# Banded attention with a mixture of experts: pair outputs scaled in place in PSUM, two small steps given to ScalarE, operand turns placed behind later filler pieces

## The chip, the cores and the metric

The kernel runs on one core of a Trainium2 chip. The metric is the time of one execution in microseconds on the device. The runs of the kernel before gave 2286.73 us (median of 3; 2285.66 to 2288.38).

The engines are named as the profile names them: PE is TensorE (PEld its weight loads), DVE is VectorE, ACT is ScalarE, POOL is GpSimd, SP is SyncE. A matrix product leaves its result in PSUM; SBUF is the other on-chip memory.

## The reference, cut to what matters

```python
def _attn_ref(q, k, v, n_global, n_local):        # q, k, v: 4 x 8 x 768 x 64; n_global 8, n_local 96
    scores = q @ k^T / sqrt(D) + bias(head, distance)      # masked to a band of 96 keys and 8 global keys
    scores = scores - max(scores, axis=-1)
    a = exp(scores)
    a = a / (sum(a, axis=-1) + 1e-09)
    return a @ v

def _moe_ref(x, w_gate, w1, w2):                  # x: 3072 x 512; 8 experts, 512 x 1024 x 512 each
    logits = x @ w_gate
    P = exp(logits - logits.max())
    for _ in range(8):                            # Sinkhorn: rows, then columns, are brought to one sum
        P /= P.sum(1) + 1e-09; P /= P.sum(0) + 1e-09; P *= N / E
    return sum(P[:, e:e+1] * (relu(x @ w1[e]) @ w2[e]) for e in range(8))
```

## The kernel before, in words

The first 380 us or so are the attention stage, in eight units of 384 query rows. A unit holds four pairs of heads, a pair three tasks (one block of 128 query rows for both heads), and the code goes through the tasks two at a time, as a chunk. In a chunk (`Banded.unit`, L352 on) PE gets, in an order that is fixed by hand: the scores of the two tasks that lie four and five ahead (`ahead`, `scores`), the value products of the two tasks of the chunk before (`flush`), the transposes of two softmax blocks (`turn`, tiles `t_ps`), and then pieces of other work. `between(n)` puts in pieces of the dense first expert for the unit before (`filler`, three matmuls each into `h_ps` or `y_ps`, and the gate into `g_ps`); unit 0 has none. Between the pieces stand two calls of `prepare` (the operand turns: tiles `tp`, transposes of raw queries and keys, split by L239 on ACT into a high part `qh`/`kh` and by L240 on DVE into a low part `ql`/`kl`) and, in two chunks of three, `invert` (tile `r_ps`, transposes of the pair's inverse sums, read back by L393 on DVE). All of `tp`, `t_ps` and `r_ps` take turns in two PSUM buffers.

Outside PE the order is set by the scheduler of the framework; each engine runs its list strictly in order.

After the third task of a pair, `softmax` makes the inverse sums: add epsilon to six sums per partition (L294, DVE), reciprocal (L295, DVE), spread them to 128x384 (L297, DVE). When a pair's value products are done, `flush` scales them (L382, DVE, out of PSUM into the SBUF tile `inv`), takes the high part (L384, ACT, from SBUF) and the low part (L385, DVE, both inputs in SBUF). There are 32 pairs, so each of these lines runs 32 times.

The gate's logits leave PSUM by L719 and L720 (DVE), once for each of the units 0 to 6 in this stage; the matmul piece behind them waits for the buffer.

On POOL, `sums_of` and `differences` combine the finished units of a pair of units: 25 instructions of 128x768 in a row, three times (once for units 0 and 1, once for 2 and 3, once for 4 and 5). After the attention stage follows the mixture of experts, on PE nearly without a gap, to the end.

The change touches `softmax`, `unit` and `flush`. The functions with their line numbers:

Of the kernel before, what the change touches and what calls it, by code (L numbers as in the profile page):

```python
# [12 lines left out]
ALU = mybir.AluOpType  # L13
# [4 lines left out]
P = 128  # L18
# [4 lines left out]
EPS = 1e-9  # L23
UT = 3
# [4 lines left out]
AHEAD = 4  # L29
CHUNK = 2  # L30
# [58 lines left out]
class Banded:  # L89
# [178 lines left out]
    def softmax(self, t, s_list):  # L268


        nc, D = self.nc, self.D
        n, group = divmod(t, len(GROUPS))
        _, half, g = self.work[n]
        blocks = self.key_blocks(half)[1]
        p_sb = self.wrk.tile([P, 2, 2, P], F32, name="p_sb")
        mx = self.wrk.tile([P, 2], F32, name="mx", bufs=4)
        if group == 0:
            self.sums[n] = self.wrk.tile([P, UT, 2], F32, name="sm", bufs=4)
        sm = self.sums[n]
        views = []  # L280
        for u, (j, i) in enumerate(GROUPS[group]):
            h = 2 * g + j
            nb = len(blocks[i])
            bias = self.bias0[:, h] if nb == 1 else self.bias1[:, h]
            pv = p_sb[:, u, 0:nb].rearrange("p a c -> p (a c)")
            views.append(pv)
            nc.vector.tensor_tensor_reduce(out=pv, in0=s_list[u], in1=bias, scale=-(D ** -0.5), scalar=3.0e38,
                                           op0=ALU.add, op1=ALU.min, accum_out=mx[:, u:u + 1])
        for u, pv in enumerate(views):
            j, i = GROUPS[group][u]  # L290
            nc.scalar.activation(out=pv, in_=pv, func=AF.Exp, bias=mx[:, u:u + 1], scale=-1.0,
                                 accum_out=sm[:, i, j:j + 1])
        if group == len(GROUPS) - 1:
            nc.vector.tensor_scalar(out=sm, in0=sm, scalar1=EPS, scalar2=None, op0=ALU.add)  # L294
            nc.vector.reciprocal(out=sm, in_=sm)  # L295
            self.inv[n] = self.wrk.tile([P, UT, P], F32, name="inv", bufs=3)
            nc.vector.tensor_copy(self.inv[n].rearrange("p t (j d) -> p (t j) d", j=2),  # L297
                                  sm.rearrange("p t j -> p (t j)").unsqueeze(2).broadcast_to([P, 2 * UT, D]))
        return p_sb

    def blocks(self, n, group):
# [28 lines left out]
    def unit(self, u, xh, xl, between):  # L330

        NG, per = len(GROUPS), len(GROUPS) * (self.H // 2)
        if u == 0:
            self.load_qk(1)
            self.load_v(1)
            for t in range(NG):
                self.prepare(t)
            self.scale_bias(0)  # L340
            self.keep_warm(self.ps, "o", WARM0)
            self.ahead(range(0, CHUNK))
            for t in range(NG, 2 * NG):
                self.prepare(t)
            for g in range(1, self.H // 2):
                self.scale_bias(g)
            for t in range(CHUNK, AHEAD, CHUNK):
                self.ahead(range(t, t + CHUNK))
            for t in range(2 * NG, AHEAD + NG + 1):
                self.prepare(t)  # L350
        for t in range(u * per, (u + 1) * per, CHUNK):
            self.ahead(range(t + AHEAD, t + AHEAD + CHUNK))  # L352
            self.flush()
            turned = [(t + c, self.turn(t + c)) for c in range(CHUNK)]
            between(CHUNK)
            for c in range(CHUNK):
                self.prepare(t + AHEAD + NG + 1 + c)
                between(1)
            for t1, pT in turned:
                n, group = divmod(t1, NG)  # L360
                if group == NG - 1:
                    self.invert(n)
                if group == 0:
                    self.outs[n] = self.ps.tile([P, UT, P], F32, name="o_ps", tag="o", bufs=2)
                g = n % (self.H // 2)
                self.pending.append((n, group, pT, self.outs[n], xh[:, g], xl[:, g]))

    def flush(self):


        ended = None
        for n, group, pT, o_ps, xh, xl in self.pending:
            self.values(n, group, pT, o_ps)
            if group == len(GROUPS) - 1:
                ended = n, o_ps, xh, xl
        self.pending = []
        if ended is None:
            return
        n, o_ps, xh, xl = ended
        self.load_v(n + 2)  # L380
        xf = self.inv.pop(n)
        self.nc.vector.tensor_tensor(out=xf, in0=o_ps, in1=xf, op=ALU.mult)  # L382
        xf = xf.rearrange("p t c -> p (t c)")
        self.nc.scalar.copy(out=xh, in_=xf)  # L384
        self.nc.vector.tensor_tensor(out=xl, in0=xf, in1=xh, op=ALU.subtract)  # L385

    def invert(self, n):

# [645 lines left out]
```

## Time and profile before

| | |
|---|---|
| runs of the kernel | 2286.73 us median of 3 (2285.66 to 2288.38) |
| the profiled execution | 2288.16 us |
| its span, first to last instruction | 2286.3 us |
| PE busy | 2236.0 us (98%) |
| DVE busy | 1560.3 us (68%) |
| ACT busy | 696.2 us (30%) |
| POOL busy | 823.5 us (36%) |
| mean granted TensorE clock | 0.989 |

The busy shares are means over two stages that differ. The page's picture of 40 slices shows it: ACT is busy 4 to 6 tenths in the first seven slices and 2 in the others, and the clock is below 9 tenths only in the first slice. In the rows below, a number in brackets behind an instruction is the idle time of its engine just before it and what ended that. A clock of 1.00 is 2.4 GHz, of 0.50 is 1.2 GHz.

### The profile page before, as it was taken

The numbers are of one execution on the slowest core, as the hardware profiler recorded it, in microseconds if no ns is written. First come the engines' busy times: TensorE is split into PE (matmuls) and PEld (weight loads), VectorE is DVE, ScalarE is ACT, GpSimd is POOL, SyncE is SP. The second block draws the span as 40 slices with busy tenths as digits, with TensorE's granted clock in tenths as the row PEclk, the third lists the DMA queues.
The fourth block names the chain that finished last, engine by engine and source line by source line (L and its number), as shares of the span: only waits on it lengthen the run. The fifth ranks groups of instructions, "written<-read, shape, count | busy, mean of one in ns | idle before, by whom it ended". The sixth has DMA issues, their size and how long they took to land.

```text
span 2286.3 us, 31486 instructions
## 1 busy us (share of the span) xinstructions
PE 2236.0 (98%) x12147; PEld 1991.2 (87%) x12147; DVE 1560.3 (68%) x2746; ACT 696.2 (30%) x1528; POOL 823.5 (36%) x655
## 2 busy tenths in 40 slices
PE   7989989999999999999999999999999999999998
PEld 5777878898998998998998998998998999989987
DVE  6566666886766666766666667666766666666665
ACT  5655654332222222222222224222222222222221
POOL 4165283432333333333333234333333233333320
PEclk8999999999999999999999999999999999999999
DMA  6455433110111011111001361101110101110101
GB/s 163 116 163 145 125 85 95 32 43 28 37 38 38 28 30 36 38 37 37 28 29 38 129 239 39 36 28 38 37 38 28 37 28 38 37 37 28 35 22 57
DMA packets 177615, 133.75 MB, mean 59 GB/s; under 512 B 117040, under 2 KB 148784, under 8 KB 177456
## 3 DMA queue, kind: packets, MB, share of 16 engines
q1 hardware_dynamic: 177456, 131.65, 19.3%
q8 instruction: 97, 1.59, 0.3%
q14 instruction: 62, 0.51, 0.1%
HBM read 108.81 MB, written 22.81 MB: 58 GB/s over the span
## 4 chain that ended last, share of the span: by engine, by line
PE 90%; DVE 3%; issue 3%; POOL 2%; ACT 1%; DMA 0%; SPq 0%; DVEq 0%; POOLq 0%; ACTq 0%
PE y_ps L686 15%; PE y_ps L687 15%; PE y_ps L685 14%; PE bank_d L618 4%; PE bank_d L617 4%; PE bank_c L617 4%; PE bank_c L619 4%; PE bank_a L618 4%; PE bank_c L618 4%; PE bank_a L617 4%; PE bank_d L619 4%; PE bank_a L619 4%; PE bank_b L617 2%; PE bank_b L619 2%; PE bank_b L618 2%
## 5 line engine op out<-in xcount | busy, mean ns | idle before, releaser
L937 DVE SCALAR_TENSOR_TENSOR acc<-y_ps,pm,acc 128x512 f32<-128x512 f32 x672 | 500.2, 748 | 327.0 <-PE y_ps L687 324.5
L687 PE MATMUL y_ps<-w2h,hh 128*128 128x512 f32 x1440 | 567.5, 394 | 0.0
L686 PE MATMUL y_ps<-w2h,hl 128*128 128x512 f32 x1440 | 566.9, 394 | 0.0
L685 PE MATMUL y_ps<-w2l,hh 128*128 128x512 f32 x1440 | 561.9, 390 | 0.0
L538 POOL TENSOR_TENSOR w2l<-w2f,w2h 128x1024 fp32r<-128x1024 f32 x60 | 144.5, 2408 | 702.0 <-ACT w2h L537 702.0
L687 PEld LDWEIGHTS y_ps<-w2h,hh 128*128 128x128 f32 x1440 | 270.1, 188 | 53.7
L685 PEld LDWEIGHTS y_ps<-w2l,hh 128*128 128x128 f32 x1440 | 270.4, 188 | 43.5 <-DVE acc L937 0.2
L686 PEld LDWEIGHTS y_ps<-w2h,hl 128*128 128x128 f32 x1440 | 270.0, 188 | 43.4
L560 POOL TENSOR_TENSOR wsum<-w1f 128x256 f32<-128x256 f32 x300 | 225.5, 786 | 216.5 <-DMA w1f<-in_moe_w_dram 216.5
L538 POOL TENSOR_TENSOR wl<-wsum,wh 128x1280 fp32r<-128x1280 f32 x60 | 177.4, 2957 | 279.4 <-ACT wh L537 279.4
L625 ACT ACTIVATE hh<-h 128x384 fp32r<-128x384 f32 x120 | 63.1, 526 | 502.5 <-DVE h L665 501.1
L626 DVE SCALAR_TENSOR_TENSOR hl<-t,hh 128x384 fp32r<-128x384 f32 x120 | 165.1, 1376 | 10.2 <-ACT hh L625 10.1
L617 PE MATMUL bank_d<-xl,wh 128*128 128x384 f32 x480 | 160.9, 335 | 1.5 <-DVE t L671 1.5
L617 PE MATMUL bank_c<-xl,wh 128*128 128x384 f32 x480 | 161.9, 337 | 0.0
L619 PE MATMUL bank_c<-xh,wh 128*128 128x384 f32 x480 | 161.9, 337 | 0.0
L618 PE MATMUL bank_c<-xh,wl 128*128 128x384 f32 x480 | 161.2, 336 | 0.0
L618 PE MATMUL bank_d<-xh,wl 128*128 128x384 f32 x480 | 161.2, 336 | 0.0
L618 PE MATMUL bank_a<-sh,wl 128*128 128x384 f32 x480 | 161.1, 336 | 0.0
L617 PE MATMUL bank_a<-sl,wh 128*128 128x384 f32 x480 | 161.0, 335 | 0.0
L619 PE MATMUL bank_a<-sh,wh 128*128 128x384 f32 x480 | 160.8, 335 | 0.0
L619 PE MATMUL bank_d<-xh,wh 128*128 128x384 f32 x480 | 160.3, 334 | 0.0
L626 DVE SCALAR_TENSOR_TENSOR hl<-h,hh 128x384 fp32r<-128x384 f32 x120 | 110.1, 918 | 68.7 <-ACT hh L625 68.7
(195 smaller groups left out, 3960.1 us busy)
## 6 DMA issues: line engine op xcount, KB each, us to landing
w1f<-in_moe_w_dram SPq DMA_DIRECT2D x62, 512.0 KB, 3.4
w2f<-in_moe_w_dram SPq DMA_DIRECT2D x62, 512.0 KB, 3.7
out_dram<-acc SPq DMA_DIRECT2D x24, 256.0 KB, 2.2
ys<-y_sb SPq DMA_DIRECT2D x21, 256.0 KB, 2.1
acc<-ys SPq DMA_DIRECT2D x7, 768.0 KB, 4.3
acc<-in_q_dram SPq DMA_DIRECT2D x32, 96.0 KB, 2.5
acc<-in_k_dram SPq DMA_DIRECT2D x32, 96.0 KB, 2.7
acc<-in_v_dram SPq DMA_DIRECT2D x32, 96.0 KB, 2.2
```

The costliest lines, as they stand in the source:

```text
L538: self.nc.gpsimd.tensor_tensor(out=lo, in0=full, in1=hi, op=ALU.subtract)
L560: nc.gpsimd.tensor_tensor(out=s[:, n], in0=x, in1=y, op=op)
L617: self.pe.matmul(out, lhsT=hi(c), rhs=xlo(c), start=(first and c == 0), stop=False, skip_group_check=True)
L618: self.pe.matmul(out, lhsT=lo(c), rhs=xhi(c), start=False, stop=False, skip_group_check=True)
L619: self.pe.matmul(out, lhsT=hi(c), rhs=xhi(c), start=False, stop=(last and c == n - 1), skip_group_check=True)
L625: nc.scalar.activation(out=hh, in_=src, func=AF.Relu)
L626: self.latest = nc.vector.scalar_tensor_tensor(out=hl, in0=src, scalar=0.0, in1=hh, op0=ALU.max, op1=ALU.subtract)
L685: self.pe.matmul(y_ps, lhsT=hh[:, cols], rhs=lf, start=(f == 0), stop=False)
L686: self.pe.matmul(y_ps, lhsT=hl[:, cols], rhs=wf, start=False, stop=False)
L687: self.pe.matmul(y_ps, lhsT=hh[:, cols], rhs=wf, start=False, stop=(f == n - 1))
L937: nc.vector.scalar_tensor_tensor(out=a, in0=y_ps, scalar=moe.pm[:, tt, e:e + 1], in1=a, op0=ALU.mult, op1=ALU.add)
```

## The change

Three edits. In `softmax` the addition of epsilon and the spreading of the inverse sums go from DVE to ACT; the reciprocal stays on DVE. In `flush` the product with the inverse sums is written back into the PSUM tile `o_ps`, and both halves of the split read it from there. In `unit` the two calls of `prepare` stand behind `invert` and behind one more piece each.

```diff
@@ softmax
-            nc.vector.tensor_scalar(out=sm, in0=sm, scalar1=EPS, scalar2=None, op0=ALU.add)
+            nc.scalar.add(sm, sm, EPS)
             nc.vector.reciprocal(out=sm, in_=sm)
             self.inv[n] = self.wrk.tile([P, UT, P], F32, name="inv", bufs=3)
-            nc.vector.tensor_copy(self.inv[n].rearrange("p t (j d) -> p (t j) d", j=2),
-                                  sm.rearrange("p t j -> p (t j)").unsqueeze(2).broadcast_to([P, 2 * UT, D]))
+            nc.scalar.copy(out=self.inv[n].rearrange("p t (j d) -> p (t j) d", j=2),
+                           in_=sm.rearrange("p t j -> p (t j)").unsqueeze(2).broadcast_to([P, 2 * UT, D]))
@@ unit
             turned = [(t + c, self.turn(t + c)) for c in range(CHUNK)]
             between(CHUNK)
-            for c in range(CHUNK):
-                self.prepare(t + AHEAD + NG + 1 + c)
-                between(1)
             for t1, pT in turned:
...
                 self.pending.append((n, group, pT, self.outs[n], xh[:, g], xl[:, g]))
+            for c in range(CHUNK):
+                between(1)
+                self.prepare(t + AHEAD + NG + 1 + c)
@@ flush
-        xf = self.inv.pop(n)
-        self.nc.vector.tensor_tensor(out=xf, in0=o_ps, in1=xf, op=ALU.mult)
-        xf = xf.rearrange("p t c -> p (t c)")
-        self.nc.scalar.copy(out=xh, in_=xf)
-        self.nc.vector.tensor_tensor(out=xl, in0=xf, in1=xh, op=ALU.subtract)
+        self.nc.vector.tensor_tensor(out=o_ps, in0=o_ps, in1=self.inv.pop(n), op=ALU.mult)
+        of = o_ps.rearrange("p t c -> p (t c)")
+        self.nc.scalar.copy(out=xh, in_=of)
+        self.nc.vector.tensor_tensor(out=xl, in0=of, in1=xh, op=ALU.subtract)
```

From L385 on, the line numbers of the kernel after are smaller by one (L240 and L295 keep theirs; the scaling is L381, the high part L383, the low part L384, the read-back of the inverse sums L392, the logits L718 and L719, the low part of an expert's hidden values L625).

What this makes of the engines' lists is shown at three places. The first is DVE in the chunk of unit 1 in which the gate's logits leave PSUM, from the end of one pair on (the same seven times in the stage). Before:

```order
L382 TENSOR_TENSOR inv<-o_ps,inv 128x384
L294 TENSOR_SCALAR sm<-sm 128x6
L295 RECIPROCAL sm<-sm 128x6
L297 COPY inv<-sm 128x384
L385 TENSOR_TENSOR xl<-inv,xh 128x384
L719 COPY lg<-gt_ps 128x24
L720 TENSOR_TENSOR lg<-gt_ps,lg 128x24
L626 SCALAR_TENSOR_TENSOR hl<-h_ps,hh 128x384
L240 TENSOR_TENSOR ql<-tp,qh 128x384
L240 TENSOR_TENSOR kl<-tp,kh 128x512
L393 COPY inv<-r_ps 128x384
```

And with the change:

```order
L381 TENSOR_TENSOR o_ps<-o_ps,inv 128x384
L384 TENSOR_TENSOR xl<-o_ps,xh 128x384
L295 RECIPROCAL sm<-sm 128x6
L392 COPY inv<-r_ps 128x384
L718 COPY lg<-gt_ps 128x24
L625 SCALAR_TENSOR_TENSOR hl<-h_ps,hh 128x384
L719 TENSOR_TENSOR lg<-gt_ps,lg 128x24
L240 TENSOR_TENSOR ql<-tp,qh 128x384
L240 TENSOR_TENSOR kl<-tp,kh 128x512
```

Two instructions are gone, the read-back of the inverse sums stands ahead of the logits, and `hl` between their two halves (in the built program the next piece on PE waits for this `hl`, where it waited for the second half).

The second place is PE in the same chunk, from the last matmul of a piece to the next scores. Before:

```order
L83 MATMUL h_ps<-xh,w1h 128x384
L86 MATMUL tp<-ident,acc 128x128 x3
L86 MATMUL gt_ps<-ident,g_sb 128x16 x3
L83 MATMUL h_ps<-xl,w1h 128x384
L83 MATMUL h_ps<-xh,w1l 128x384
L83 MATMUL h_ps<-xh,w1h 128x384
L86 MATMUL tp<-ident,acc 128x128 x4
L83 MATMUL h_ps<-xl,w1h 128x384
L83 MATMUL h_ps<-xh,w1l 128x384
L83 MATMUL h_ps<-xh,w1h 128x384
L86 MATMUL r_ps<-ident,inv 128x128 x3
```

And with the change:

```order
L83 MATMUL h_ps<-xh,w1h 128x384
L86 MATMUL r_ps<-ident,inv 128x128 x3
L86 MATMUL gt_ps<-ident,g_sb 128x16 x3
L83 MATMUL h_ps<-xl,w1h 128x384
L83 MATMUL h_ps<-xh,w1l 128x384
L83 MATMUL h_ps<-xh,w1h 128x384
L86 MATMUL tp<-ident,acc 128x128 x3
L83 MATMUL h_ps<-xl,w1h 128x384
L83 MATMUL h_ps<-xh,w1l 128x384
L83 MATMUL h_ps<-xh,w1h 128x384
L86 MATMUL tp<-ident,acc 128x128 x4
```

The transposes of the inverse sums have changed places with the operand turns, and the last turn stands right ahead of the scores.

The third place is PE one chunk earlier, in front of scores of which the second task reads keys that were turned in this chunk (16 chunks of 48 are of this kind). Before:

```order
L86 MATMUL t_ps<-ident,p_sb 128x128 x8
L86 MATMUL tp<-ident,raw_745 128x128 x4
L83 MATMUL g_ps<-xl,ghl 128x384
...
L83 MATMUL g_ps<-xh,ghl 128x384
L86 MATMUL tp<-ident,raw_745 128x128 x2
L83 MATMUL h_ps<-xl,w1h 128x384
L83 MATMUL h_ps<-xh,w1l 128x384
L83 MATMUL h_ps<-xh,w1h 128x384
L86 MATMUL r_ps<-ident,inv 128x128 x3
L83 MATMUL s_ps_1042<-kl,qh 128x256
```

And with the change:

```order
L86 MATMUL t_ps<-ident,p_sb 128x128 x8
L86 MATMUL r_ps<-ident,inv 128x128 x3
L83 MATMUL g_ps<-xl,ghl 128x384
...
L83 MATMUL g_ps<-xh,ghl 128x384
L86 MATMUL tp<-ident,raw_751 128x128 x4
L83 MATMUL h_ps<-xl,w1h 128x384
L83 MATMUL h_ps<-xh,w1l 128x384
L83 MATMUL h_ps<-xh,w1h 128x384
L86 MATMUL tp<-ident,raw_751 128x128 x2
L83 MATMUL s_ps_1042<-kl,qh 128x256
```

The turn of four key blocks has moved behind the gate's piece; one piece and a turn of two blocks are left between it and the scores. In the built program the seventh score matmul waits for the `kl` of the four-block turn, not for that of the two-block one.

From the end of the attention stage on, the lists of all engines are the same but for a few neighbours in the first tens of microseconds.

## Rows read from the trace of the kernel before

**Rows 1.** Busy time by stage (PE, PEld, DVE, ACT, POOL; clock, DMA).

```profile
20.00:80.00 60.00, 47.06 (x380) 37.35 (x379) 38.86 (x125) 36.37 (x114) 17.83 (x15) 0.85 0.62 154
80.00:380.00 300.00, 276.18 (x2230) 237.21 (x2229) 191.84 (x552) 174.03 (x517) 141.95 (x77) 0.95 0.46 124
380.00:2286.00 1906.00, 1898.33 (x9473) 1709.07 (x9471) 1317.15 (x2015) 477.95 (x876) 653.16 (x539) 1.00 0.14 45
```

**Rows 2.** The same view, stretches of the attention stage with and without POOL.

```profile
105.00:153.00 48.00, 40.52 (x315) 34.43 (x315) 34.00 (x84) 24.46 (x75) 46.40 (x25) 0.90 0.58 171
153.00:198.00 45.00, 44.42 (x377) 38.47 (x374) 26.60 (x96) 30.02 (x92) 0.03 (x1) 0.99 0.48 127
...
290.00:338.00 48.00, 40.45 (x315) 34.57 (x315) 33.96 (x83) 24.27 (x74) 46.35 (x25) 0.90 0.31 75
```

**Rows 3.** Who PE waited for, 80 to 380 us (us in total, times, longest).

```profile
PE h_ps L83 <- DVE lg L720: 12.2, 6, 3.5
PE r_ps L86 <- DVE ql L240: 5.6, 3, 2.0
PE t_ps L86 <- DVE kl L240: 4.3, 3, 2.0
```

**Rows 4.** DVE in order of time, 300.5 to 307 us, POOL busy (start, us).

```profile
300.56 1.01 DVE L294 TENSOR_SCALAR sm<-sm 128x6 f32<-128x6 f32 x1 [0.31 <-ACT p_sb L291]
...
301.82 1.70 DVE L297 COPY inv<-sm 128x384 f32<-128x384 f32 x1
303.44 2.15 DVE L385 TENSOR_TENSOR xl<-inv,xh 128x384 fp32r<-128x384 f32 x1
...
305.82 0.55 DVE L626 SCALAR_TENSOR_TENSOR hl<-h_ps,hh 128x384 fp32r<-128x384 f32 x1
```

**Rows 5.** DVE in order of time, 168.6 to 170.6 us, POOL idle.

```profile
168.63 0.17 DVE L294 TENSOR_SCALAR sm<-sm 128x6 f32<-128x6 f32 x1
...
169.06 0.36 DVE L297 COPY inv<-sm 128x384 f32<-128x384 f32 x1
170.00 0.56 DVE L385 TENSOR_TENSOR xl<-inv,xh 128x384 fp32r<-128x384 f32 x1 [0.58 <-ACT xh L384]
```

**Rows 6.** PE in order of time: two of the gaps under POOL.

```profile
243.01 0.55 PE L86 MATMUL r_ps<-ident,inv 128*128 128x128 f32 x3 [1.54 <-DVE ql L240]
...
306.05 0.66 PE L83 MATMUL h_ps<-xl,w1h 128*128 128x384 f32 x1 [3.48 <-DVE lg L720]
```

**Rows 7.** Busy time and clock (the last but two numbers: clock) around and behind them.

```profile
240.00:250.00 10.00, 8.46 (x67) 6.51 (x67) 8.05 (x20) 6.06 (x18) 5.83 (x4) 1.00 0.81 217
...
306.05:312.00 5.95, 5.95 (x39) 5.26 (x41) 2.68 (x7) 0.77 (x2) 5.87 (x4) 0.57 0.00 0
334.55:340.00 5.45, 5.45 (x42) 4.65 (x43) 3.76 (x14) 2.82 (x10) 2.97 (x2) 0.69 0.05 12
```

**Rows 8.** Groups of instructions by line, 20 to 380 us (count, busy us, mean ns).

```profile
L384 ACT CAST xh<-inv 128x384 fp32r<-128x384 f32 x32 | 16.4, 512 | 5.2 <-DVE inv L382 5.2
```

**Rows 9.** PE and DVE in order of time, 162.5 to 166 us: a turn and the scores behind.

```profile
162.52 0.60 PE L86 MATMUL tp<-ident,raw 128*128 128x128 f32 x4
162.88 0.42 PE L83 MATMUL g_ps<-xl,ghl 128*128 128x384 f32 x1
...
163.83 0.69 DVE L240 TENSOR_TENSOR kl<-tp,kh 128x512 fp32r<-128x512 f32 x1 [3.08 <-ACT kh L239]
...
164.37 0.38 PE L86 MATMUL tp<-ident,raw 128*128 128x128 f32 x2
...
165.11 0.49 PE L86 MATMUL r_ps<-ident,inv 128*128 128x128 f32 x3
165.53 0.39 PE L83 MATMUL s_ps<-kl,qh 64*128 64x256 f32 x2
...
165.99 0.28 PE L83 MATMUL s_ps<-kl,qh 64*128 64x256 f32 x2
```

**Rows 10.** PE in order of time in unit 0: its longest wait.

```profile
30.77 0.73 PE L86 MATMUL tp<-ident,raw 128*128 128x128 f32 x4 [2.80 <-ACT acc L313]
```

## The prediction

> **What bounds the kernel now.** I read the busy time by stage first. From 380 us to the end PE is busy for 1898.33 of 1906 us at a clock of 1.00, while the attention stage before it leaves PE free for 12.94 us of the stretch 20 to 80 us and for 23.82 us of the stretch 80 to 380 us, with clocks of 0.85 and 0.95 [rows 1]. So the end is set by PE, the change can pay only ahead of 380 us, and what it saves there is carried to the end, since the lists behind are nearly the same.
>
> Where in the stage PE stands still, the shorter stretches show. In the two stretches with 25 POOL instructions PE is free for 48 − 40.52 = 7.48 us and 48 − 40.45 = 7.55 us; in the 45 us between two such stretches, with POOL idle, for 0.58 us [rows 2]. The waits of PE give the same picture by partner: 12.2 + 5.6 + 4.3 = 22.1 us behind DVE, in 12 waits [rows 3], which is 7.4 us for each of the three POOL runs.
>
> DVE in order of time shows why DVE is late. With POOL busy L294 takes 1.01, L297 1.70 and L385 2.15 us [rows 4]; with POOL idle they take 0.17, 0.36 and 0.56 us [rows 5]. That is 4.86 us against 1.09, 3.77 us more for a pair. All three read only SBUF. The low part of an expert's hidden values, of the size of L385 but with one input in PSUM, takes 0.55 us in the same POOL run [rows 4], so it isn't slowed. The longest PE gap, 3.48 us, ends behind exactly this sequence [rows 6].
>
> After a long gap the clock is lower too. Behind the gap of 3.48 us PE is busy throughout at 0.57, so partly at the 1.2 GHz level, and behind a later one of the same run at 0.69; around the gap of 1.54 us it stays at 1.00 [rows 6, 7].
>
> **The change part by part.** *Epsilon and spreading on ScalarE, scaling in place.* L294 and L297 leave DVE. L384, the subtraction, has one input in PSUM now and should take 0.55 us under POOL, as the hidden values' row does [rows 4]. DVE is then not slowed at these places, and PE's 22.1 us of waits [rows 3] go: **+22.1 us**. Bounds: nothing goes, if something else makes DVE late, or all of it. I take all, as PE loses only 0.58 us where DVE isn't slowed [rows 2].
>
> *The clock behind the gaps.* In one POOL run 5.95 us × 0.43 + 5.45 us × 0.31 = 4.25 us of full-speed work are lost [rows 7]; three runs give **+12.7 us**. As a bound from above, all of the stage's loss past 80 us is 276.18 × 0.05 = 13.8 us [rows 1]; from below it is nothing, if new waits of over 1.54 us come.
>
> *The price on ACT.* For each of 32 pairs L297 costs about 0.51 us (ACT's 128x384 copy out of SBUF, L384, takes 512 ns [rows 8]) and L294 between DVE's 0.17 us [rows 5] and that 0.51; I take 0.2, as it has six elements per partition. 0.71 × 32 = 22.7 us in all. The cover: ACT is busy for 24.46 of 48 us under POOL and for 30.02 of 45 without [rows 2], so I cost it at nothing. Without that cover it would be 22.7 us, which is a rival below. L384, the high part, becomes L383 with PSUM as its source; ACT's reads from there are of the same kind as the L239 it does all along, and I cost the difference at nothing. The PSUM bank `o_ps` is held until L384 has read it, an ACT and a DVE instruction longer; it has two buffers and is wanted again a pair later, so this is hidden.
>
> The Trainium skill has a rule against this part: "ScalarE: Activation LUTs", section "Rules for kernel authors", sends additions and multiplications to VectorE and not to ScalarE, as the faster engine for them. The trace agrees with POOL idle (0.36 us against ACT's 512 ns [rows 5, 8]) and not with POOL busy (1.70 us [rows 4]).
>
> *The gate's logits.* `hl` now stands between L718 and L719 and behind the read-back of `r_ps`, and the next piece waits for it. Behind `gt_ps` come 0.55 us (read-back, priced as the 128x384 read from PSUM [rows 4]) + 0.17 (L718, as L294's small tile [rows 5]) + 0.55 (`hl` [rows 4]) = 1.27 us. Seven times that is 8.9 us, against 0.58 us [rows 2] in the four quiet units before (the three under POOL are already in the 22.1): 8.9 − 2.3 gives **−6.6 us**. Bounds: nothing, if the read-back is done by the time `gt_ps` ends; and 7 × 1.54 = 10.8, the wait of [rows 6] that keeps the clock.
>
> *The operand turns behind later pieces.* In 16 chunks the seventh score matmul reads keys of the four-block turn. From the start of that turn to the end of `kl` it takes 163.83 + 0.69 − 162.52 = 2.00 us [rows 9]. What PE does meanwhile, after the change: the turn itself 0.36 (162.52 to 162.88), the two-block turn and the piece 0.74 (164.37 to 165.11), six score matmuls 0.46 (165.53 to 165.99) [rows 9], together 1.56. So 0.44 us are uncovered; in the 14 such chunks outside unit 0 that is **−6.2 us**. Before, the gate's piece and the transposes of inverse sums were cover as well. Bounds: nothing to 2.0 us per chunk. In exchange `r_ps` comes first, where it needs what the first operand turn needed (a free buffer, read by ACT's L313), so it waits no longer than that did.
>
> *Unit 0.* It has no filler. Its longest PE wait, 2.80 us [rows 10], stands behind DVE work of the slowed lines; L294 and L297 leave DVE there too, but ACT, busy for 36.37 of 60 us [rows 1], takes some 5 pairs × 0.71 = 3.5 us. Bounds: −3.5 us, and the wait plus the clock's 47.06 × 0.15 = 7.1 us [rows 1], together 9.9. I take **+2.8 us**, the wait alone.
>
> **Sum:** 22.1 + 12.7 − 6.6 − 6.2 + 2.8 = 24.8 us. The profiled execution took 2288.16 us, so it would be 2263.4; it lies 1.43 us above the median of the runs, 2286.73, and the forecast for the median is **2261.9 us**. With the bounds of the two new waits (0 to 10.8 for the logits, and half to double the 6.2) and of unit 0 it lies between 2253 and 2273.
>
> **The rivals.** *A: no new wait comes.* If the turns' latency and the logits are hidden, and unit 0 gains most of its bound, 22.1 + 12.7 + 6 = 40.8 us, so 2246 us. For it: the quiet stretch shows almost no waits [rows 2]. Against it: the order now leaves only 1.56 us for a 2.00 us chain [rows 9]. Chance 0.10.
>
> *B: ScalarE sets the pace.* All 22.7 us of its new work lands on the path: 24.8 − 22.7 leaves 2 us, so 2284.6 us. For it: ACT is the engine that PE's transposes wait for in unit 0 [rows 10]. Against it: 30.02 of 45 us busy [rows 2]. Chance 0.07.
>
> *C: the in-place product doesn't free DVE.* If L384, with `xh` in SBUF, is still blocked by POOL, only L294's and L297's excess goes (0.84 + 1.34 = 2.18 of 3.77 us, 58% [rows 4, 5]). 0.58 × 34.8 − 12.8 + 2.8 gives 10 us, so 2276.7 us. For it: `xh` and `xl` are in SBUF as before. Against it: the hidden values' subtraction has the same kinds of operands and takes 0.55 us [rows 4]. Chance 0.12.
>
> On the last point the Trainium skill, "SBUF — State Buffer", section "Who interferes with whom", says that a DVE instruction contends with GpSimd when it has two SBUF inputs (and GpSimd reads SBUF) or runs in a two-port mode, and not with a single SBUF input otherwise. By that rule rival C is out, and the rows agree: 2.15 us with two SBUF inputs, 0.55 with one [rows 4].
>
> *D, slower: the turns right ahead of the scores stall PE.* If in the 16 chunks ACT's and DVE's lists bring the wait from 0.44 to 2 us (the whole chain of [rows 9] uncovered), that is 32 us, and such gaps bring the clock down (4.25 us for two of them [rows 7], so 2.1 us each, 34 us): 24.8 + 6.2 − 66 = −35 us, so 2322 us. It turns to a loss from about 1.9 us per chunk without the clock (31.0 / 16), earlier with it. For it: `kl` waits for `kh` on ACT [rows 9], where two more instructions per pair now stand. Against it: the piece and the first six score matmuls still lie between. Chance 0.06.
>
> **How the numbers follow.** The forecast has 0.65. The range reaches from A (2246) to a little past C (2279) and leaves out B, D and what lies beyond, under 2 in 10. A measurement of this kernel can tell about 0.2%, 4.6 us, from no change. Faster by more than that: forecast, A and C, 0.87. Within: B, 0.07. Slower: D, 0.06.
>
> **What would show it.** Right: under POOL the subtraction L384 takes about 0.55 us and no PE gap of 3.5 us is left; the stretches of [rows 2] show PE free for some 3 us instead of 7.5 and a clock near 1.00; ACT's copy L297 takes about 0.5 us. PE waits for `kl` in the middle of the scores (0.4 us, 14 times) and for `hl` or `lg` behind `gt_ps` (1.3 us, 7 times). Wrong: L384 at 2 us (C); PE waiting for ACT's copies outside unit 0 (B); gaps of 2 us ahead of the scores and a clock below 0.9 in the quiet stretch too (D). POOL's own instructions, and everything past 380 us, should be as before.

## The result, and the profile after

The changed kernel takes 2260.98 us (median of 4 runs, 2260.31 to 2262.83) against 2287.53 us beside it: 0.9883 of the time of before, 95% interval 0.9871 to 0.9896, so 26.55 us less. The forecast was 2261.9 us, 24.8 us less than 2286.73 us, the median of the three runs that it knew. The profiled execution took 2260.31 us, with a span of 2258.5 us where it was 2286.3 us.

The busy time by stretches of the changed kernel (PE, PEld, DVE, ACT, POOL; then clock, DMA share, GB/s), to be held against [rows 1, 2]:

```profile
20.00:80.00 60.00, 48.19 (x423) 38.66 (x422) 33.31 (x124) 42.42 (x137) 17.40 (x15) 0.91 0.65 161
80.00:353.00 273.00, 265.36 (x2197) 227.55 (x2196) 143.07 (x491) 185.75 (x560) 141.25 (x77) 1.00 0.50 136
353.00:2258.00 1905.00, 1896.41 (x9462) 1707.27 (x9460) 1313.49 (x2015) 477.20 (x874) 650.31 (x539) 1.00 0.14 44
...
105.00:153.00 48.00, 46.52 (x382) 39.79 (x380) 25.14 (x86) 33.79 (x103) 42.54 (x24) 1.00 0.68 202
153.00:198.00 45.00, 43.55 (x375) 37.34 (x372) 23.16 (x87) 30.51 (x97) 11.41 (x7) 1.00 0.50 130
...
290.00:338.00 48.00, 46.97 (x393) 40.78 (x392) 24.54 (x84) 33.70 (x103) 26.60 (x15) 1.00 0.41 109
```

Under POOL, PE was free for 7.48 us of the stretch 105 to 153 us [rows 2]; now it is for 1.48 us, and the clock is 1.00 where it was 0.90. Without POOL it has become a little worse: 1.45 us free of 45 instead of 0.58 [rows 2] (this stretch now holds the beginning of a POOL run). DVE and ACT have changed places: under POOL DVE went from 34.00 to 25.14 us, ACT from 24.46 to 33.79.

The waits of PE from 80 to 380 us, against [rows 3] (us in total, times, longest):

```profile
PE h_ps L83 <- DVE hl L625: 5.7, 6, 1.0
PE bank_c L616 <- ACT t L657: 1.6, 1, 1.6
PE s_ps L83 <- DVE kl L240: 1.0, 3, 0.3
```

DVE of the changed kernel in order of time, in the chunk that answers to [rows 4], with POOL busy:

```profile
280.85 0.56 DVE L381 TENSOR_TENSOR o_ps<-o_ps,inv 128x384 f32<-128x384 f32 x1
282.94 0.56 DVE L384 TENSOR_TENSOR xl<-o_ps,xh 128x384 fp32r<-128x384 f32 x1 [1.53 <-ACT xh L383]
283.48 0.56 DVE L392 COPY inv<-r_ps 128x384 f32<-128x384 f32 x1
283.96 0.17 DVE L718 COPY lg<-gt_ps 128x24 f32<-128x24 f32 x1
284.05 0.18 DVE L295 RECIPROCAL sm<-sm 128x6 f32<-128x6 f32 x1
284.14 0.51 DVE L625 SCALAR_TENSOR_TENSOR hl<-h_ps,hh 128x384 fp32r<-128x384 f32 x1
284.58 0.17 DVE L719 TENSOR_TENSOR lg<-gt_ps,lg 128x24 f32<-128x24 f32 x1
```

The subtraction takes 0.56 us where it took 2.15 [rows 4]. From its start to the start of `hl` DVE now needs 1.20 us (282.94 to 284.14), with the read-back of the inverse sums in it. Before, from L294 on, it needed 5.26 us to the same place (300.56 to 305.82 [rows 4]). In exchange DVE is idle for 1.53 us ahead of the subtraction, until ACT has made the high part.

ACT in the same chunk shows the two steps that it was given:

```profile
282.43 0.47 ACT L383 CAST xh<-o_ps 128x384 fp32r<-128x384 f32 x1
...
283.27 0.22 ACT L294 ACTIVATE sm<-sm 128x6 f32<-128x6 f32 x1
283.38 0.49 ACT L624 ACTIVATE hh<-h_ps 128x384 fp32r<-128x384 f32 x1
284.26 0.51 ACT L297 COPY inv<-sm 128x384 f32<-128x384 f32 x1 [0.39 <-DVE sm L295]
```

They cost 0.22 and 0.51 us, the forecast's 0.2 and 0.51, and no PE wait outside unit 0 is put down to them.

**Where the 27.8 us of span come from.** A ruler that both kernels share is the transposes of the gate's logits (`gt_ps`), once in each unit. Before, PE in order of time:

```profile
117.64 0.35 PE L86 MATMUL gt_ps<-ident,g_sb 16*128 16x16 f32 x3
170.40 0.35 PE L86 MATMUL gt_ps<-ident,g_sb 16*128 16x16 f32 x3
210.66 0.35 PE L86 MATMUL gt_ps<-ident,g_sb 16*128 16x16 f32 x3
```

and after:

```profile
114.81 0.35 PE L86 MATMUL gt_ps<-ident,g_sb 16*128 16x16 f32 x3
157.16 0.36 PE L86 MATMUL gt_ps<-ident,g_sb 16*128 16x16 f32 x3
199.07 0.35 PE L86 MATMUL gt_ps<-ident,g_sb 16*128 16x16 f32 x3
```

A unit under POOL went from 52.76 to 42.35 us, the next one, whose own work POOL hardly delays, from 40.26 to 41.91. All the units read in this way (us; the first column is the start of the first `gt_ps`, the last but one runs to the transpose of the gate's maximum, `gmt_ps`):

| kernel | to first | quiet | POOL | quiet | POOL | quiet | POOL | to `gmt_ps` | to the end |
|---|---|---|---|---|---|---|---|---|---|
| before | 77.36 | 40.28 | 52.76 | 40.26 | 51.25 | 40.31 | 52.44 | 48.62 | 1883.02 |
| after | 72.90 | 41.91 | 42.35 | 41.91 | 42.36 | 41.95 | 42.34 | 47.62 | 1885.16 |
| e1, order kept | 75.70 | 40.26 | 41.72 | 40.29 | 41.74 | 40.29 | 41.41 | 47.60 | 1885.19 |
| e2, order alone | 78.04 | 41.70 | 49.44 | 41.71 | 51.29 | 41.69 | 49.43 | 48.66 | 1883.14 |
| e3, ScalarE alone | 75.14 | 40.27 | 44.68 | 40.27 | 44.64 | 40.27 | 44.28 | 48.71 | 1883.04 |
| e4, PSUM alone | 77.43 | 40.26 | 43.31 | 40.26 | 45.23 | 40.29 | 44.93 | 47.63 | 1885.26 |
| e5, POOL only writes | 78.30 | 40.29 | 42.33 | 40.26 | 42.35 | 40.25 | 42.02 | 48.68 | 1883.72 |
| e7, inverses first | 74.26 | 40.40 | 41.95 | 40.44 | 41.97 | 40.45 | 41.33 | 47.64 | 1885.76 |

From before to after: 4.5 us in unit 0, 29.4 us in the three units under POOL, −4.9 us in the three quiet ones, and −1.1 us behind them (1.0 − 2.1).

### The profile page after: what moved, and what is told of

It reads as the page before. It is cut to its first block, busy times and chain, and to the rows that moved or that the text cites. A ratio compares the mean times of both kernels' runs of the same rounds, so it can differ in the third digit from the quotient of the medians.

```text
span 2258.5 us, 31464 instructions
## 1 busy us (share of the span) xinstructions
PE 2224.2 (98%) x12147; PEld 1981.0 (88%) x12147; DVE 1501.7 (66%) x2682; ACT 712.9 (32%) x1592; POOL 819.5 (36%) x655
## 4 chain that ended last, share of the span: by engine, by line
PE 91%; ACT 3%; DVE 2%; issue 2%; POOL 1%; DMA 0%; SPq 0%; ACTq 0%; DVEq 0%; POOLq 0%
PE y_ps L685 15%; PE y_ps L686 15%; PE y_ps L684 15%; PE bank_d L617 4%; PE bank_d L616 4%; PE bank_c L616 4%; PE bank_c L618 4%; PE bank_a L617 4%; PE bank_c L617 4%; PE bank_d L618 4%; PE bank_a L616 4%; PE bank_a L618 4%; PE bank_b L616 2%; PE bank_b L618 2%; PE bank_b L617 2%
## 5 line engine op out<-in xcount | busy, mean ns | idle before, releaser
L625 DVE SCALAR_TENSOR_TENSOR hl<-t,hh 128x384 fp32r<-128x384 f32 x120 | 165.4, 1378 | 9.9 <-ACT hh L624 9.8
L625 DVE SCALAR_TENSOR_TENSOR hl<-h,hh 128x384 fp32r<-128x384 f32 x120 | 111.2, 927 | 68.7 <-ACT hh L624 68.7
```

The costliest lines, as they stand in the source:

```text
L625: self.latest = nc.vector.scalar_tensor_tensor(out=hl, in0=src, scalar=0.0, in1=hh, op0=ALU.max, op1=ALU.subtract)
```

## The experiments

**e1 to e4: the parts apart.** e1 keeps both arithmetic edits and puts the turns back:

```diff
             between(CHUNK)
+            for c in range(CHUNK):
+                self.prepare(t + AHEAD + NG + 1 + c)
+                between(1)
             for t1, pT in turned:
...
-            for c in range(CHUNK):
-                between(1)
-                self.prepare(t + AHEAD + NG + 1 + c)
```

> Both arithmetic edits of the change (epsilon and spreading on ScalarE, scaling in place in PSUM), with the operand turns left where they were before. Theory (POOL was the cause, the new order only costs): the units without POOL take 40.3 us from one gate transpose to the next, as before, and not the 41.9 us of the change; with 1.64 us saved in seven units the time is about 2261.0 - 11.5 = 2249.5 us, and PE's only regular wait is the 0.6 us for the gate's logits. Rival (the new order gives the engines the slack that keeps PE fed under POOL): the units with POOL get waits of 1 us or more back and the time is 2261 us or above.

Measured: 2256.87 us, 0.9853 of before (0.9839 to 0.9866). The quiet units are back at 40.3 us, as the theory said, and the rival's waits under POOL didn't come (41.7 us against 42.35). But the time fell by 4.1 us and not by 11.5. The table says why: the late turns cost a unit under POOL only 0.6 us (0.9 in the last one, which holds three transposes more in the changed kernel), and with them unit 0 is 2.8 us shorter (75.70 against 72.90), which the expectation had left out. In the six units between the first and the last `gt_ps` the late order costs 7.1 us.

e2 is the kernel before with the turns moved as in the change's diff, and nothing else.

> Only the operand turns are moved, the arithmetic is that of before. Theory: the waits behind DVE under POOL stay (gaps of 2 to 3.5 us, clock 0.9 in these stretches), and the quiet units lengthen from 40.3 to 41.9 us, so it is slower than before: 2287 + 7 x 1.64 = about 2298 us, from 2292 to 2304. Rival (the order is what feeds PE): at least a third of the 27 us comes with it, 2278 us or below.

Measured: 2291.03 us, 1.0009 of before (0.9997 to 1.0020): no difference that this comparison can tell. Both expectations missed. The quiet units do lengthen to 41.7 us, but two of the three units under POOL get shorter (49.4 us). In these two the transposes of the inverse sums, which now stand ahead of the turns, no longer wait 2.02 us each for `ql`, and the clock is 0.97 where it was 0.90; in the third a new wait of 0.80 us, of a turn for the read-back, takes the place of the 1.54 us, and its length is unchanged (51.29 against 51.25). The rival's third of the gain is not there.

e3 makes only the edit of `softmax`, e4 only that of `flush`.

> Only epsilon and spreading go to ScalarE; the subtraction keeps two SBUF inputs. Theory (each SBUF-only DVE line is slowed by POOL, and a gap of up to about 1.5 us leaves the clock up): 2.18 of the 3.77 us per pair go, the longest gap falls from 3.5 to some 1.3 us, so the clock stays at 1.00 and the gain is 12.8 (gaps) + about 12 (clock), 2262 us, from 2257 to 2268; the subtraction still takes 2.1 us under POOL. Rival (what matters is the subtraction, the last in the row): little changes, 2280 us or above.

Measured: 2265.5 us, 0.9892 (0.9876 to 0.9907), as the theory said. The subtraction is still slow under POOL, and the gap in front of the piece behind the logits is 1.64 us; DVE and PE of e3 in order of time, and the clock behind two such gaps (the last number but two):

```profile
284.88 1.94 DVE L385 TENSOR_TENSOR xl<-inv,xh 128x384 fp32r<-128x384 f32 x1 [1.58 <-ACT xh L384]
...
117.40 0.41 PE L83 MATMUL h_ps<-xl,w1h 128*128 128x384 f32 x1 [1.64 <-DVE lg L720]
...
287.27 0.41 PE L83 MATMUL h_ps<-xl,w1h 128*128 128x384 f32 x1 [1.65 <-DVE lg L720]
...
117.40:121.00 3.60, 3.60 (x38) 3.23 (x40) 2.53 (x7) 1.00 (x3) 3.44 (x3) 1.00 0.88 275
287.27:291.00 3.73, 3.73 (x19) 3.27 (x21) 2.03 (x4) 0.87 (x2) 3.57 (x3) 0.60 0.23 53
```

Two gaps of the same length, and the clock stayed at 1.00 behind one and was 0.60 behind the other. So part of the clock's loss stays, in two of the three units under POOL. All three take 44.3 to 44.7 us, those of e1 41.4 to 41.7; the longer gaps are the other part of that.

> Only the scaling in place; epsilon and spreading stay on DVE. Theory: the subtraction takes 0.55 us under POOL and 1.6 of the 3.77 us per pair go; the longest gap falls to some 1.9 us, which lies where the clock still fell in the run before, so gaps give 9.4 us and the clock a part, 0 to 12 us: 2266 to 2278 us. Rival (the subtraction does not speed up, since its other operand and its result are in SBUF): 2285 us, and the row shows 2 us under POOL.

Measured: 2265.88 us, 0.9890 (0.9875 to 0.9906), just below the theory's range. DVE of e4 under POOL:

```profile
285.12 0.66 DVE L294 TENSOR_SCALAR sm<-sm 128x6 f32<-128x6 f32 x1 [0.30 <-ACT p_sb L291]
...
286.04 1.71 DVE L297 COPY inv<-sm 128x384 f32<-128x384 f32 x1
287.67 0.54 DVE L384 TENSOR_TENSOR xl<-o_ps,xh 128x384 fp32r<-128x384 f32 x1
```

The subtraction is free of POOL at 0.54 us, although `xh` and `xl` still lie in SBUF, so that rival falls; L294 and L297 aren't free. The two halves alone save about 23 us each, and together (e1) 32, not 46: either one shortens the longest gap from 3.5 to some 1.6 us, and with that removes most of what the gaps and the clock cost.

**e5: what it is about POOL.** The kernel before; POOL's combines in the attention stage write zeros and read nothing but two columns:

```diff
-            nc.gpsimd.tensor_tensor(out=s, in0=x[0], in1=y[0], op=op)
-            nc.gpsimd.tensor_tensor(out=dst[0], in0=s, in1=r, op=ALU.add)
-            nc.gpsimd.tensor_tensor(out=s, in0=s, in1=r, op=ALU.add)
-            nc.gpsimd.tensor_tensor(out=dst[1], in0=s, in1=dst[0], op=ALU.subtract)
+            one = slice(0, 1)
+            nc.gpsimd.tensor_tensor(out=r[:, :, one], in0=x[1][:, :, one], in1=y[1][:, :, one], op=op)
+            for _ in range(6):
+                nc.gpsimd.memset(r, 0.0)
+            for i in range(2):
+                nc.gpsimd.tensor_tensor(out=dst[i][:, :, one], in0=x[i][:, :, one], in1=r[:, :, one], op=op)
+                nc.gpsimd.memset(dst[i].bitcast(F32), 0.0)
```

> The kernel before, in which POOL's combines of finished units in the attention stage are left out and replaced by fills with zero of the same tiles (eight of 128x768 per combine, which read nothing; three additions of two columns per combine keep their place in the order). It leaves out the sums of units, so the experts' result is another. Theory by kind of operand: the subtraction (L385, two SBUF inputs) is slowed only by a POOL that reads, so it is back at about 0.6 us, while the addition of epsilon and the spreading (L294, L297, one SBUF input and SBUF output) still take 1.0 and 1.7 us or more wherever POOL is filling. Rival (any POOL work slows all three alike): L385 stays near 2 us under POOL. Second rival (none of the three is slowed by fills): all three as with POOL idle.

Measured, in a single run: 2260.03 us (before beside it 2288.98). The groups of POOL (100 to 230 us) and DVE (20 to 370 us) by line (count, busy us, mean ns):

```profile
L611 POOL MEMSET xres<- 128x768 f32 x60 | 44.5, 742 | 3.5
...
L297 DVE COPY inv<-sm 128x384 f32<-128x384 f32 x32 | 20.6, 644 | 1.1
L385 DVE TENSOR_TENSOR xl<-inv,xh 128x384 fp32r<-128x384 f32 x32 | 17.7, 555 | 6.5 <-ACT xh L384 5.4
...
L294 DVE TENSOR_SCALAR sm<-sm 128x6 f32<-128x6 f32 x32 | 9.4, 294 | 16.5 <-ACT p_sb L291 15.9
```

and DVE in order of time, with POOL filling:

```profile
125.80 1.69 DVE L297 COPY inv<-sm 128x384 f32<-128x384 f32 x1
127.41 0.54 DVE L385 TENSOR_TENSOR xl<-inv,xh 128x384 fp32r<-128x384 f32 x1
```

The subtraction is never slowed (its longest of 32 is 0.56 us), the spreading beside it still takes 1.69 us. So the theory by kind of operand holds: two SBUF inputs are slowed by a POOL that reads, the copy and the addition by a POOL that only writes too. For the addition the expected size was not reached: it took 0.77 us once in each run of POOL, not 1.0 or more. The total is a weaker witness, since the fills also keep POOL busy for a shorter time (from 107 to 141 us in the first run, 34 us instead of 48).

The Trainium skill, "SBUF — State Buffer", section "Who interferes with whom", draws this line: two SBUF inputs contend with a GpSimd instruction that reads SBUF and not with one that only writes; copies and `tensor_scalar` can run in a two-port mode, and that contends with GpSimd without this condition. The rows of e4 (0.54 us with one SBUF input) and e5 (0.54 and 1.69 us) agree.

**e6 and e7: which part of the order costs.** e6 was to keep the late turns in unit 0 only, where there is no filler:

```diff
-            for c in range(CHUNK):
+            for c in range(CHUNK if u else 0):
                 self.prepare(t + AHEAD + NG + 1 + c)
                 between(1)
...
+            for c in range(0 if u else CHUNK):
+                self.prepare(t + AHEAD + NG + 1 + c)
```

> Both arithmetic edits; the operand turns stand behind the transposes of the inverse sums in unit 0 only (it has no filler pieces), and where they were before in all other units. Theory (the late turns gain 2.8 us in unit 0 and cost 0.6 to 1.65 us in each later unit): 2256.9 - 2.8 = about 2254 us; the first gate transpose at about 73 us, units of 40.3 and 41.7 us. Rival (unit 0 gains by something else than the order): 2257 us, the first gate transpose at 75.7 us.

Measured: 2264.85 us, 0.9896 (0.9880 to 0.9912), which neither expected, and the first `gt_ps` came at 92.12 us. The edit did more than it says: `between` also counts slots, in unit 0 too, and by that count the pieces fall due. With 12 calls fewer (of unit 0's 24 slots) all pieces of filler came later, and the last ones were done behind the attention stage. So it tells nothing on unit 0.

e7 puts the transposes of the inverse sums first in all units, with each turn ahead of its piece and no call left out:

```diff
-            for c in range(CHUNK):
-                between(1)
-                self.prepare(t + AHEAD + NG + 1 + c)
+            for c in range(CHUNK):
+                self.prepare(t + AHEAD + NG + 1 + c)
+                between(1)
```

(against the changed kernel, at the same place).

> Both arithmetic edits; the transposes of the inverse sums come first in all units, and each operand turn has its filler piece behind it, as before, not ahead of it. Theory (of the 1.65 us that the change costs a unit without POOL, 0.33 us come from the gate's logits behind the read-back and the rest from the turns' distance to the scores): units without POOL take about 40.6 us, unit 0 is as short as with the change (73 us), so 2261.0 - 7 x 1.0 = about 2254 us. Rival (it is the place of the read-back that costs): units without POOL stay at 41.5 us or more, 2260 us.

Measured: 2254.47 us, 0.9852 (0.9834 to 0.9871); the changed kernel on the same chip (e8) 2260.97, 0.9882 (0.9866 to 0.9899). The quiet units fall from 41.9 to 40.4 us, the theory's 40.6. But the edit does two things. It takes away what the turns' distance had cost: the twelve score matmuls that read fresh keys start within 1.05 and 1.22 us in a quiet unit of the changed kernel and within 0.64 us in e7 and e1 (0.90 and 1.07 against 0.70 us under POOL), 4.7 us in the six units. And as the first turn now stands between `r_ps` and `gt_ps`, DVE has more time for `hl`. PE of e7, and its list of waits from 80 to 380 us:

```profile
155.55 0.49 PE L86 MATMUL r_ps<-ident,inv 128*128 128x128 f32 x3
156.13 0.55 PE L86 MATMUL tp<-ident,acc 128*128 128x128 f32 x3
156.61 0.35 PE L86 MATMUL gt_ps<-ident,g_sb 16*128 16x16 f32 x3
157.16 0.44 PE L83 MATMUL h_ps<-xl,w1h 128*128 128x384 f32 x1 [0.20 <-DVE hl L625]
...
PE h_ps L83 <- DVE hl L625: 2.4, 6, 0.9
```

The changed kernel waits 5.7 us at this place, and e1 3.5 us (six waits of 0.58 to 0.60 for the logits). So the fall to 40.4 us does not separate turns and read-back, and the theory's split is not shown by it (what the two give is more than the 6.3 us that the six units gain; e7 loses some of it in small pieces elsewhere in PE's list). e1 separates them better, since its order is that of before: of the 7.1 us that the late order costs, 4.7 lie between the score matmuls and 2.2 behind `gt_ps`, in a quiet unit 1.00 and 0.34 of 1.64 (the theory's 0.33 for the logits). The ratios of e7 and e1 can't be told apart (0.9852 and 0.9853). Unit 0 keeps a part of its gain (74.26; e8 gave 73.58 for the changed kernel, so 0.7 us is within its scatter).

> The changed kernel once more, beside the other two versions on the same chip: 2261 us; the units of the attention stage as in its first profile.

**e9: the logits later.** The gate's logits are taken 12 pieces behind the gate and not 4, on top of e7:

```diff
-                for _ in range(KT):
+                for _ in range(3 * KT):
                     yield next(rest)
                 yield from gate
```

> The kernel of e7 (both arithmetic edits, transposes of the inverse sums first, a piece behind each operand turn), with the gate's logits taken 12 pieces behind the gate instead of 4, so that the scores and values of a chunk lie between the last piece of one tile of hidden values and the transposes of the logits. Theory (the wait of 0.6 to 0.9 us for the logits comes from the low part of the hidden values not being done): the wait goes, units without POOL take about 39.7 us, and the time is 2254.5 - 7 x 0.7 = about 2249.5 us. Rival (the wait only moves, since the next tile of hidden values still follows the logits at once): 40.4 us a unit, 2254 us.

Measured: 2251.2 us, 0.9836 of before (0.9821 to 0.9850): the interval of its ratio ends below that of the changed kernel, and overlaps with those of e1 and e7. From the first product of one gate (`g_ps`) to that of the next a unit takes 40.8 us where e7 takes 41.0 or 41.4, so the wait was worth 0.4 us a unit rather than 0.7: the theory's 0.6 to 0.9 us are the waits of e1 and of the changed kernel, those of e7 were mostly 0.2 to 0.35 already. The stretch behind unit 0 of e9:

```profile
80.00:350.00 270.00, 269.47 (x2228) 230.28 (x2227) 150.62 (x494) 185.45 (x558) 148.28 (x81) 1.00 0.52 142
```

PE is busy for 269.47 of 270 us at a clock of 1.00. There is next to nothing left to take from waits there; what is left lies in unit 0 and at the hand-over to the next stage.

## Why the prediction was right, point by point

**The mechanism and the sum.** The forecast, 24.8 us, met 26.55 us (27.8 us by the spans). Its main reason, DVE slowed by POOL and the clock behind it, is what e1 to e5 show; that the sum came so close is in part luck. It took 3.2 us too much for the gain and 5.9 us too much for the price of the two new waits, 1.7 us too little for unit 0, and it left out 1.1 us at the end of the stage. Its narrower range, 2253 to 2273, is also less than what its bounds add up to (2245 to 2279). The terms:

- *Waits behind DVE and the clock, +22.1 and +12.7 = 34.8 us.* By the units under POOL, e1 against before, 156.45 − 124.87 = 31.6 us. The difference is the wait behind the logits. Of the 22.1 us 1.7 us are its three waits of 0.58 us in the quiet units, which e1 still has (and which the logits' term subtracts once more), and e1 keeps 0.58 us in each unit under POOL too. Less both the forecast was 31.4. PE's busy time in these units, where the clock shows, fell from 134.39 to 122.75 us, 11.6 us for the forecast's 12.7. The clock is 1.00 from 80 us on, as forecast.
- *ACT's price, nothing.* 0.22 and 0.51 us per pair, hidden outside unit 0: PE waits for neither there. ACT is busy for 33.79 of 48 us. Rival B is out.
- *The gate's logits, −6.6 us.* Right in place, mis-sized: PE waits for `hl` for 0.95 us and not 1.27 (5.7 us in 6 waits). What is new of it is less still, since e1 waits there too, in all units: 5.7 against 3.5 us, so −2.2 us. Two things were sized wrong. The read-back was counted in full behind `gt_ps`, but a part of it runs while `gt_ps` is on PE (it starts at 283.48 us, `gt_ps` at 283.38 and lasts 0.35). And the 0.58 us of before was set against the new wait only in the four quiet units.
- *The turns' distance, −6.2 us.* The mechanism came, at 4.7 us in the 12 such chunks between the first and the last `gt_ps`, 0.39 us each. (Changed kernel against e7 is 6.3 us, but that holds the shorter wait for `hl` as well.) In the list of waits only 1.0 us stands under `kl`, in three waits. The rest is in shorter pauses. The forecast's 0.44 us was worked out for the kind of chunk with a two-block turn and taken for all. In the quiet units these chunks have no two-block turn in front of the scores, so there is less cover; PE after:

```profile
194.25 0.28 PE L83 MATMUL s_ps<-kh,qh 64*128 64x256 f32 x2
194.85 0.33 PE L83 MATMUL s_ps<-kl,qh 64*128 64x128 f32 x2 [0.33 <-DVE kl L240]
```

  From the sixth to the seventh score matmul 0.60 us pass, where the step before it took 0.12: some 0.48 us lost, of which the list of waits shows 0.33. In a chunk of the kind of the third excerpt of the change, with the two-block turn, 0.39 us pass (152.27 to 152.66), some 0.27 us lost, and the list shows nothing.
- *Unit 0, +2.8 us.* 4.5 us in the first profile, 3.8 in e8. The size was luck in part. The wait of 2.80 us that the term took as gone [rows 10] is not gone in the first profile; it stands ahead of the transposes of the inverse sums, which have taken the turn's place, behind the same copy on ACT:

```profile
28.54 0.55 PE L86 MATMUL r_ps<-ident,inv 128*128 128x128 f32 x3 [2.19 <-ACT acc L313]
```

  It ends 2.23 us earlier than before (30.77 to 28.54); in e8 the wait is 0.37 us. e1 has 1.7 of the 4.5 us (its arithmetic). What the order adds has no one cause that the runs show: up to the first `gt_ps` PE is idle for 16.66 us in the first profile of the changed kernel, 14.17 in e8 and 16.39 in e1, and busy for 56.24, 59.41 and 59.31 us, at mean clocks of 0.91, 0.86 and 0.86. So the first profile is ahead of e1 by its clock, e8 by shorter waits. e2 shows that the order alone gives nothing in unit 0 (78.04).
- *What the sum had left out, −1.1 us.* Behind the attention stage the lists were taken as alike. They aren't quite. POOL before:

```profile
384.66 2.56 POOL L601 TENSOR_TENSOR xres<-xl 128x768 f32<-128x768 f32 x1
387.19 3.11 POOL L538 TENSOR_TENSOR w2l<-w2f,w2h 128x1024 fp32r<-128x1024 f32 x1
391.19 1.84 POOL L601 TENSOR_TENSOR xres<-xl 128x768 f32<-128x768 f32 x1 [0.89 <-DVE xsum L604]
392.99 6.37 POOL L560 TENSOR_TENSOR wsum<-w1f 128x256 f32<-128x256 f32 x5
```

  and after, with the first wait of PE that follows from it:

```profile
355.71 3.11 POOL L537 TENSOR_TENSOR w2l<-w2f,w2h 128x1024 fp32r<-128x1024 f32 x1
358.77 2.57 POOL L600 TENSOR_TENSOR xres<-xl 128x768 f32<-128x768 f32 x1
361.30 5.67 POOL L559 TENSOR_TENSOR wsum<-w1f 128x256 f32<-128x256 f32 x5
366.93 1.83 POOL L600 TENSOR_TENSOR xres<-xl 128x768 f32<-128x768 f32 x1
...
375.23 0.44 PE L616 MATMUL bank_c<-xl,wh 128*128 128x384 f32 x1 [1.62 <-ACT t L657]
```

  The scheduler has put the weights' low half and the five sums of weights ahead of one `xres` each. The units' last combine, and behind it ACT's copy for PE, come later. The table has the same step (47.6 us, and 1885.2 to 1885.8) in each of the kernels with the in-place scaling that have its columns (after, e1, e4, e7), and not in before, e2, e3 and e5. So it comes with the in-place scaling; that the POOL order is its cause follows from these rows, but wasn't tried by itself.

**The rivals.** A (2246 us) needed no new waits; e9, which removes them all behind unit 0, is at 2251.2. B is out by the terms above, C by e4. D did not come: the uncovered part stayed at 0.2 to 0.6 us per chunk, and the clock at 1.00; the piece and six score matmuls still lie between turn and use.

## What to carry to other kernels

Before costing an operation on VectorE, look what GpSimd does at that moment: here three SBUF-only lines took 4.9 us instead of 1.1 while it ran, and the same work with one operand left in PSUM, or on a ScalarE that had room, took none of that. An order of work that hides one wait should be costed chunk by chunk apart from the edits it comes with: here it gave back 7 us of 32 behind unit 0, some 4 us in all, and setting only the turns ahead of their pieces again won as much back. A run that undoes one edit can move a second wait with it, as e7 did, so read its list of waits before its time is put down to one cause. After each edit read the hand-over to the next stage too: a scheduler may reorder it after an edit in another place.

## What the runs showed that was not expected

The length of a gap alone doesn't say whether the granted clock falls. Gaps of 1.64 and 1.65 us at the same place of two units of e3 left it at 1.00 and at 0.60, and the gap of 1.54 us of before left it at 1.00 [rows 6, 7]. The forecast took the last for a bound, which it isn't: in e4 a gap of the same 1.54 us stands ahead of a clock of 0.61.

```profile
288.67 0.41 PE L83 MATMUL h_ps<-xl,w1h 128*128 128x384 f32 x1 [1.54 <-DVE lg L719]
...
288.67:293.00 4.33, 4.33 (x25) 3.84 (x25) 2.03 (x4) 0.59 (x1) 4.17 (x3) 0.61 0.20 45
```

The two halves of the arithmetic don't add up: about 23 us each alone, 32 together.
